# Pooled attention into a feed-forward layer: attention values with tokens in rows and a DMA transpose of x, instead of features in rows

## The chip, the core and the metric

The kernel runs on one core of one Trainium2 chip. The metric is the device time of one execution in microseconds. A core has TensorE (PE, matmul; its weight loads are listed apart as PEld), VectorE (DVE), ScalarE (ACT), GpSimd (POOL), and SyncE (SP), which here only issues DMAs. Matmul results land in PSUM; everything else that the engines read and write lies in SBUF. Sixteen DMA engines move data between the main memory and SBUF, and within SBUF.

## The reference

`q`, `k`, `v` are float32 of shape (8 batches, 8 heads, 576 tokens, 64). Keys and values are averaged over groups of 8 tokens, so each query attends to 72 pooled positions. The attended heads are laid side by side as `x` (4608 tokens x 512) and go through a feed-forward layer with an unusual gate.

```python
k_p = k.reshape(B, H, Sp, pool, D).mean(axis=3)      # pool = 8, Sp = 72
v_p = v.reshape(B, H, Sp, pool, D).mean(axis=3)
scores = scale * np.matmul(q, k_p.transpose(0, 1, 3, 2))
scores = scores - np.max(scores, axis=-1, keepdims=True)
attn = np.exp(scores)
attn = attn / (np.sum(attn, axis=-1, keepdims=True) + 1e-09)
x = np.matmul(attn, v_p)            # then heads side by side: (4608, 512)
h = x @ w_in                        # (4608, 2048)
out = (h * np.cos(h)) @ w_out       # (4608, 512)
```

## The kernel before

**Stages.** The feed-forward layer works on tiles of 512 tokens, the attention on batches of 576. A loop over t = 0..8 (L524) does for tile t the *up* part (x times `w_in`, L317), the gate h cos h (cosine on ACT at L327, product on DVE at L331) and the *down* part (times `w_out`, L395), and between the pieces of the down part the attention of batch b = t + 1. Since a tile is shorter than a batch, the attention runs ahead of the tiles by an amount that shrinks by 64 tokens a stage. The last 64 tokens of a batch (`REST`) are done one stage later than the others. In stage t = 0 down and attention are interleaved by an older list; from t = 1 on the down part is seven products (`down_products`, L367) of 16 matmuls with 256 columns each, held in the two PSUM tiles `obanks`. Batches from the third on (b = 2 to 7, stages t = 1 to 6) are what `steady` marks, and only they are touched by the change.

**Order.** The whole order is written by hand (`manual_schedule`): each engine runs its instructions in the order of the program text, and waits for what it needs. PE, ACT, DVE, POOL and SP each have one such queue. SP issues, in this order in a stage: the output rows of the tile before (8 DMAs), the transposes of q and of the pooled keys, `q_transpose` (L195) and `k_transpose` (L182). POOL issues the loads of the next batch (L95, L114), held back by a one-element copy (`gate`, L662) until the transpose of the keys has landed, and then sums groups of 8 tokens (`pool_add`, L145).

**Attention in a stage, before.** Four groups u0 to u3, each 256 tokens x 4 heads (`BY_TOKENS`), and the REST group of batch t, 64 tokens x 8 heads.

- `scores_mm` (L215): for each head a matmul with the pooled keys (64 x 72) as the stationary operand and q^T (64 x tokens) as the moving one. Heads are ordered so that two neighbours use the two halves of the array's rows. `scores_exp` (L226) takes the exponential on ACT into `ex`, 72 pooled positions x 1024 columns, in bf16. The largest score isn't subtracted.
- `values` (L245): for each head the stationary operand is `vz`, 72 x 128: 64 columns of pooled values and 64 columns that all hold the constant 8, in the order (v, 8) for even heads and (8, v) for odd ones. The moving operand is `ex`. So 64 rows of the result hold the features of the head and 64 rows hold 64 copies of the sum of the exponentials (L251, bank `pair`). ACT takes Ln of the sums (L257, twice) and Exp of minus that (L258), which is the reciprocal; DVE multiplies the two halves (L262, twice) straight into `xT`, which is x with features in rows (128 rows x 4 x 4608 tokens), as the up part needs it.

The constant is 8 since the pooled values are sums, not means, and the factor cancels.

**When xT is read.** The up part of a stage begins with the first two of the four blocks of features for its first two banks (L528, L529: `k0 = 0, k1 = 2`, 8 matmuls) and takes the other two blocks afterwards. The PSUM tiles `banks[0..2]` serve scores, values and the up part in turn.

**Shared buffers.** The reciprocals lie in the tile of `inverse_tile` (L241), 128 x 512 float32, with three buffers in turn.

Of the kernel before, what the change touches and what calls it, by code (L numbers as in the profile page):

```python
# [9 lines left out]
FP32 = mybir.dt.float32  # L10
BF16 = mybir.dt.bfloat16
# [9 lines left out]
def kernel(  # L21
# [9 lines left out]
    nc = tc.nc  # L31
    B, H, S, D = q.shape
    Sp = S // POOL
    d_model = H * D
# [3 lines left out]
    KCH = d_model // 128  # L38
# [8 lines left out]

    SEG = ((0, 256), (256, 256), (512, 64))
    REST = (SEG[2], (0, H))
    BY_TOKENS = [(SEG[s], (4 * j, 4)) for s in range(2) for j in range(2)]  # L50
    BY_HEADS = [(SEG[s], (4 * j, 4)) for j in range(2) for s in range(2)]

    ctx.enter_context(tc.manual_schedule())

# [4 lines left out]
    asb = ctx.enter_context(tc.tile_pool(name="asb", bufs=2))  # L59
# [5 lines left out]
    xT = wpool.tile([128, KCH, n_tokens], BF16, name="xT")  # L65
# [13 lines left out]
    vz = [wpool.tile([Sp, KCH, 4, D], BF16, name=f"vz{i}") for i in range(2)]  # L79
# [3 lines left out]
    banks = [psum.tile([128, 2, 512], FP32, name=f"bank{i}") for i in range(3)]  # L83
# [49 lines left out]
    att = {}  # L133
# [72 lines left out]
    def ex_col(u, i):  # L206

        (c0, n), (h0, nh) = u
        return (i // 2 % 2 * (nh // 2) + i // 4 * 2 + i % 2) * n
# [31 lines left out]
    def inverse_tile(w):  # L241
        inv = asb.tile([128, 512], FP32, name="inv", tag="inv", bufs=3)
        return inv[:, 0:w]

    def values(b, u, pair, later=None):  # L245

        (c0, n), (h0, nh) = u
        ex = att.pop(("ex", b, u))
        for i in range(nh):
            pj, hp = divmod(h0 + i, 2)  # L250
            nc.tensor.matmul(pair[:, hp, (i // 2) * n:(i // 2 + 1) * n],  # L251
                             lhsT=vz[b % 2][:, pj, 2 * hp:2 * hp + 2, :].rearrange("p a d -> p (a d)"),
                             rhs=ex[:, ex_col(u, i):ex_col(u, i) + n])
        w = nh * n // 2
        inv = inverse_tile(w)
        for hp in range(2):
            nc.scalar.activation(out=inv[half[1 - hp]], in_=pair[half[1 - hp], hp, 0:w], func=ACTF.Ln)  # L257
        nc.scalar.activation(out=inv, in_=inv, func=ACTF.Exp, scale=-1.0)  # L258

        def mul():  # L260
            for hp in range(2):
                nc.vector.tensor_mul(out=x_out(b, u, half[hp]), in0=cols(pair[half[hp], hp, :], u),  # L262
                                     in1=cols(inv[half[1 - hp]], u))

        if later is None:
            mul()
        else:
            later.append(mul)

    def sums_first(b, u, cs):  # L270

# [173 lines left out]
    for rows in half:  # L445
# [12 lines left out]
                  for x in (g1, g2)]  # L458
    groups = g3.rearrange("p f n -> p (f n)")[:, 0:ROW * Sp].rearrange("p (t n) -> p t n", t=ROW)
    nc.vector.tensor_tensor(out=dist, in0=row_of.unsqueeze(2).to_broadcast([128, ROW, Sp]),  # L460
                            in1=first_of.unsqueeze(1).to_broadcast([128, ROW, Sp]), op=mybir.AluOpType.subtract)
# [32 lines left out]
    us = BY_HEADS  # L494
# [29 lines left out]
    for t in range(NT):  # L524
        b = t + 1
        if t > 0:

            for fp in up_order(t)[0:2]:  # L528
                up_mm(t, fp, 0, 2)  # L529
        for n, fp in enumerate(up_order(t)):  # L530
            up_mm(t, fp, 2 if n < 2 else 0)
            between = ()
            if t == 0:
                if fp == 4:
                    puts = pool_k_mm(1, obanks[0], 0, 2), pool_k_mm(1, obanks[1], 2, 4)
                elif fp in (5, 6):
                    g0 = 9 * (fp - 5)
                    puts = q_transpose_mm(1, obanks[0], g0, g0 + 5), q_transpose_mm(1, obanks[1], g0 + 5, g0 + 9)
                if fp in (4, 5, 6):
                    puts[0](vec)  # L540
                    between = ((puts[1], act),)
            up_g(t, fp, between)
            if 0 < t and 3 <= n < 6:
                put_gs(*[(k, 0) for k in (((3,), (1,), ()) if t == 1 else ((1, 2), (3,), (4,)))[n - 3]])
            if 0 < t and b < B:
                if n == 0:
                    q_transpose(b)
                elif n == 2:
                    k_transpose(b)
        mms = [(ms, fc) for ms in range(4) for fc in range(FFCH)]  # L550
        if t == 0:
            mms = [(ms, fc) for hm in range(2) for cg in (0, 2, 1, 3) for ms in range(2 * hm, 2 * hm + 2)
                   for fc in range(4 * cg, 4 * cg + 4)]


        def S_(n, bank):
            return lambda: scores(b, us[n], banks[bank])

        later = []

        def V_(n, bank, wait=None):
            return lambda: values(b, us[n], banks[bank], wait)

        fill = []
        if t < B:
            exp_tables()
            fill = [(1, lambda: scores(t, REST, banks[2])), (16, lambda: values(t, REST, banks[1]))]
        if t == 0:
            fill = [(2, fill[0][1]), (2, S_(0, 0)), (8, lambda: pool_v_mm(1, banks[1])),
                    (8, lambda: values(t, REST, banks[2])), (8, S_(1, 0)), (8, V_(0, 1)),  # L570
                    (18, S_(2, 2)), (21, V_(1, 0, later)), (26, S_(3, 1)), (32, lambda: later.pop()()),
                    (32, V_(2, 2)), (40, V_(3, 0))]
        if t < FIRST:
            fi = 0
            for n, (ms, fc) in enumerate(mms):
                while fi < len(fill) and fill[fi][0] <= n:
                    fill[fi][1]()
                    fi += 1
                down_mm(obanks[ms % 2], ms, fc)
                if fc == FFCH - 1:  # L580
                    down_out(t, ms, obanks[ms % 2])
                if n == 4:
                    put_weights(0, nc.vector, (1,))
                elif n == 36:
                    put_weights(1, nc.vector, (3,))
            put_weights(1, nc.vector, (2, 4))
        else:
            products, reads = down_products(t)

            def product(i, j=0, k=2 * HF):  # L590
                for mm in products[i][j:k]:
                    mm()

            us = BY_TOKENS
            later = []

            u0, u1, u2, u3 = [(b, us[i], banks[j]) for i, j in enumerate((2, 1, 0, 1))]
            ur = (t, REST, banks[2])

            def scores_of(*parts):  # L600
                for part in parts:
                    scores_mm(*part)
                for part in parts:
                    scores_exp(*part)

            def muls():
                while later:
                    later.pop(0)()

            steady, rest = b < B, t < B  # L610
            if rest:
                exp_tables()
            product(0)
            product(1, 0, 2)
            if steady:
                scores_of(u0, u1, u2)
            elif rest:
                scores_of(ur)
            product(1, 2)
            if t == 1:  # L620
                put_g(2, 0)
            put_gs((1, 1), (2, 1))
            reads[0]()
            put_g(3, 1)
            reads[1]()
            if t == 1:
                put_g(4, 0)
            if steady:
                values(*u0, later)
            product(2)  # L630
            reads[2]()
            muls()
            if steady:
                values(*u1, later)
            product(3)
            reads[3]()
            muls()
            put_g(4, 1)
            if steady:
                values(*u2, later)  # L640
            product(4)
            reads[4]()
            muls()
            if steady:
                scores_of(ur, u3)
            product(5, 0, 4)
            if rest:
                values(*ur, later)
            product(5, 4, 12)
            muls()  # L650
            if steady:
                values(*u3, later)
            product(5, 12)
            reads[5]()
            muls()
            product(6)
            reads[6]()
        if t < B:
            sin_tables()
        if 0 < t and b + 1 < B:  # L660

            nc.gpsimd.tensor_copy(out=gate, in_=kk[b % 2][0:1, 0, 0:1])  # L662
        if b + 1 < B:
            load_kv(b + 1, "k", k)
            load_q(b + 1)
            load_kv(b + 1, "v", v)
            if t == 0:
                put_weights(0, nc.gpsimd, (3, 2, 4))
                put_weights(1, nc.gpsimd, (1,))
            pool_add(b + 1, "k")  # L670
            pool_add(b + 1, "v")
# [28 lines left out]
```

The softmax here doesn't subtract the row's maximum and nothing guards it: scores larger than these inputs give would overflow.

## Time and profile before

The time is 290.83 us, the median of 3 runs (290.38 to 291.13). The profiled execution has a span of 289.3 us at the full TensorE clock.

| Group | Engine | Count | Busy us | Mean of one, ns |
|---|---|---|---|---|
| up, 128x512 (L317, `bank`) | PE | 512 | 113.9 | 379 |
| cosine (L327, `bank`) | ACT | 64 | 70.3 | 1114 |
| gate product (L331, `bank`) | DVE | 64 | 77.2 | 1220 |
| product into xT, 64x512 (L262) | DVE | 56 | 38.6 | 689 |
| Ln of the sums, 64x512 (L257) | ACT | 56 | 33.1 | 592 |
| Exp of minus Ln, 128x512 (L258) | ACT | 28 | 17.7 | 630 |
| values, 256 columns (L251) | PE | 112 | 16.9 | 272 |
| exp of scores, 72x1024 (L229) | ACT | 32 | 31.0 | 1013 |
| scores, 256 columns (L222) | PE | 128 | 10.9 | 275 |

How to read it: the mean time of a matmul is its whole passage through the array, and the next one starts long before it ends, so the means of PE rows add up to more than the time that passes. What a matmul costs is the distance from its start to the start of the next. ACT and DVE do one instruction after the other, so their rows add up. The stages t = 2 to 6 start their up parts at 83.6, 113.8, 143.5, 173.2 and 202.9 us. In the stage from 143.47 to 173.18 us DVE is busy for 26.34 us, ACT for 24.30, POOL for 20.56.

The DMAs of SP in a stage (times are the length of the issue): output rows 8 x some 0.6 us, q transpose 2.8 us, key transpose 1.2 us; median times from issue to landing are 2.4, 4.9 and 2.8 us.

### The profile page before, as it was taken

Reading aid. Unit: us, or ns where it says so; the run is one execution under the profiler, and the core shown is the slowest. Engines: PE = TensorE matmul, PEld = TensorE weight load, DVE = VectorE, ACT = ScalarE, POOL = GpSimd, SP = SyncE. Lnnn points to the kernel's source line nnn. Section 1 sums busy time; section 2 is a strip of 40 time slices with the busy share of each in tenths; the row PEclk is TensorE's granted clock in tenths of the full one; section 3 lists DMA queues with packets and bytes.
Section 4 is the critical chain, followed back from the end, with each engine's and each line's share of the span. In section 5 each row is a group of like instructions: output and inputs, shape, how many; then the busy total and the mean of one; then the engine's idle time right before and its main releaser. Section 6 shows DMA issues by size and latency. Waiting matters only on the chain.

```text
span 289.3 us, 5446 instructions
## 1 busy us (share of the span) xinstructions
PE 281.1 (97%) x2168; PEld 178.5 (62%) x2168; DVE 233.1 (81%) x314; ACT 208.0 (72%) x265; POOL 149.9 (52%) x145
## 2 busy tenths in 40 slices
PE   7889999999999999999999999999999999999994
PEld 3545554446864587458745884588448854884583
DVE  5558747899988988798979897989798979855972
ACT  3786798378887798679967997699759976436600
POOL 8563079996698379836983599339920000000000
PEclk9999999999999999999999999999999999999999
DMA  7999999554939692969196916694670060006014
GB/s 161 194 206 207 206 205 213 116 107 58 174 72 168 99 162 42 199 92 162 19 196 95 174 31 150 109 169 71 147 106 0 5 144 1 2 5 143 0 39 109
DMA packets 44489, 32.97 MB, mean 114 GB/s; under 512 B 22192, under 2 KB 40112, under 8 KB 44464
## 3 DMA queue, kind: packets, MB, share of 16 engines
q0 software_dynamic: 19744, 18.07, 39.8%
q1 hardware_dynamic: 24080, 14.03, 23.7%
q10 hardware_dynamic: 640, 0.52, 0.7%
q8 instruction: 17, 0.28, 0.4%
q14 instruction: 8, 0.07, 0.1%
HBM read 36.70 MB, written 9.44 MB: 159 GB/s over the span
## 4 chain that ended last, share of the span: by engine, by line
PE 70%; DVE 3%; ACT 0%; issue 0%
PE obank L395 31%; PE bank L317 27%; PE bank L251 4%; PE obank L317 4%; PE bank L222 3%; DVE g_sb L331 2%; PE bank L395 2%; DVE g L361 1%; ACT cos L327 0%; DVE o_two L411 0%
## 5 line engine op out<-in xcount | busy, mean ns | idle before, releaser
L317 PE MATMUL bank<-xT,w_in_sb 128*128 128x512 bf16 x512 | 113.9, 379 | 0.0
L327 ACT ACTIVATE cos<-bank,half_pi 128x1024 f32<-128x1024 f32 x64 | 70.3, 1114 | 46.5 <-PE bank L317 46.5
L317 PEld LDWEIGHTS <-w_in_sb 128*128 128x128 bf16 x576 | 56.1, 98 | 66.0 <-issue 0.6
L331 DVE TENSOR_TENSOR g_sb<-bank,cos 128x1024 bf16<-128x1024 f32 x64 | 77.2, 1220 | 21.0 <-ACT cos L327 20.9
L151 POOL TENSOR_TENSOR half_sums<-kv_st 72x512 f32<-72x512 bf16 x48 | 54.5, 1162 | 26.2 <-DMA kv_st<-in_k_dram 25.8
L395 PEld LDWEIGHTS <-g 128*128 128x128 bf16 x512 | 49.0, 98 | 7.1 <-issue 1.4
L262 DVE TENSOR_TENSOR xT<-bank,inv 64x512 bf16<-64x512 f32 (+1 forms) x72 | 45.3, 629 | 6.8 <-ACT inv L258 5.3
L257 ACT ACTIVATE inv<-bank 64x512 f32<-64x512 f32 (+1 forms) x72 | 39.2, 544 | 10.4 <-PE bank L251 9.4
L395 PE MATMUL obank<-w,g 128*128 128x256 bf16 x368 | 43.6, 272 | 0.0
L395 PEld LDWEIGHTS <-g_sb 128*128 128x128 bf16 x384 | 36.8, 98 | 7.8 <-issue 1.2
L229 ACT ACTIVATE ex<-bank 72x1024 bf16<-72x1024 f32 (+1 forms) x40 | 35.0, 929 | 1.9 <-PE bank L222 1.7
L153 POOL TENSOR_TENSOR half_sums<-half_sums 72x512 f32<-72x512 f32 x24 | 31.8, 1345 | 0.0
L395 PE MATMUL obank<-w_out_sb,g_sb 128*128 128x256 bf16 x240 | 28.9, 273 | 0.3 <-DVE g_sb L331 0.3
L361 DVE TENSOR_TENSOR g<-g_sb 128x1024 bf16<-128x1024 bf16 x32 | 23.7, 740 | 0.5
L258 ACT ACTIVATE inv<-inv 128x512 f32<-128x512 f32 (+1 forms) x36 | 21.0, 583 | 1.1
L251 PE MATMUL bank<-ex,vz 72*128 72x256 bf16 (+1 forms) x176 | 20.0, 243 | 0.1
L156 POOL TENSOR_TENSOR kp<-half_sums 72x512 bf16<-72x512 f32 x12 | 16.4, 1389 | 0.5
L251 PEld LDWEIGHTS <-vz 72*128 72x128 bf16 x176 | 13.6, 97 | 3.5 <-DVE xT L262 0.5
L395 PE MATMUL obank<-w_out_sb,g 128*128 128x256 bf16 x112 | 15.6, 273 | 0.0
L334 PE MATMUL obank<-w_out_sb,g_sb 128*128 128x512 bf16 x64 | 15.3, 379 | 0.2 <-DMA w_out_sb<-in_moe_w_out_dram 0.2
L395 PE MATMUL obank<-w,g_sb 128*128 128x256 bf16 x128 | 15.3, 273 | 0.0
L317 PE MATMUL obank<-xT,w_in_sb 128*128 128x512 bf16 x64 | 15.1, 379 | 0.0
(85 smaller groups left out, 246.2 us busy)
## 6 DMA issues: line engine op xcount, KB each, us to landing
out_dram<-o_two SPq DMA_DIRECT2D x64, 128.0 KB, 2.4
kv_st<-in_v_dram POOLq DMA_DIRECT2D x8, 576.0 KB, 12.9
kv_st<-in_k_dram POOLq DMA_DIRECT2D x7, 576.0 KB, 7.6
q_b<-in_q_dram POOLq DMA_DIRECT2D x6, 576.0 KB, 9.9
w_in_sb<-in_moe_w_in_dram POOLq DMA_DIRECT2D x4, 512.0 KB, 13.6
w_out_sb<-in_moe_w_out_dram POOLq DMA_DIRECT2D x4, 512.0 KB, 19.0
q_b<-in_q_dram POOLq DMA_DIRECT2D x4, 288.0 KB, 12.3
g_sb<-in_k_dram SPq DMA_DIRECT2D x1, 576.0 KB, 3.6
```

Of the source, the lines that this page charges most:

```text
L151: add(out=s[:, h:h + 2], in0=x[:, h:h + 2, 0:4, :], in1=x[:, h:h + 2, 4:8, :], op=ADD)
L153: add(out=s[:, h:h + 4, 0:2, :], in0=s[:, h:h + 4, 0:2, :], in1=s[:, h:h + 4, 2:4, :], op=ADD)
L229: nc.scalar.activation(out=ex[:, 0:nh * n].rearrange("p (a n) -> p a n", a=2), in_=pair[:Sp, :, 0:nh * n // 2], func=ACTF.Exp, scale=scale ...
L251: nc.tensor.matmul(pair[:, hp, (i // 2) * n:(i // 2 + 1) * n], lhsT=vz[b % 2][:, pj, 2 * hp:2 * hp + 2, :].rearrange("p a d -> p (a d)"), ...
L257: nc.scalar.activation(out=inv[half[1 - hp]], in_=pair[half[1 - hp], hp, 0:w], func=ACTF.Ln)
L258: nc.scalar.activation(out=inv, in_=inv, func=ACTF.Exp, scale=-1.0)
L262: nc.vector.tensor_mul(out=x_out(b, u, half[hp]), in0=cols(pair[half[hp], hp, :], u), in1=cols(inv[half[1 - hp]], u))
L317: nc.tensor.matmul(h[j] if h is obanks else h[:, j, :], lhsT=w_in_sb[fc // 4][:, ki, (fc % 4) * 128:(fc % 4 + 1) * 128], rhs=xT[:, ki, t * ...
L327: nc.scalar.activation(out=c, in_=ps, func=ACTF.Sin, bias=half_pi[:, :1])
L331: nc.vector.tensor_mul(out=o, in0=ps, in1=c)
L361: nc.vector.tensor_tensor(out=out[:, f0:f1], in0=x, in1=y, op=op)
L395: mms.append(lambda bank=bank, first=first, g=g, w=w, fc=fc, p=p: nc.tensor.matmul(bank[p], lhsT=g(fc, p), rhs=w(fc), start=(first and fc ...
```

## The change

From the third batch on, the four groups are chunks of 128 tokens with all 8 heads (`CHUNKS`), and the values product is turned around: the exponentials (72 x 128 tokens) become the stationary operand, and the values of the head with *one* column of the constant (72 x 65) the moving one. The result has tokens in rows: per head 64 features and one sum. The reciprocal of the sums is then a DVE instruction over 8 columns, the division is one DVE product of 128 x 512 with the reciprocal broadcast along the features, and neither needs ACT. The price of the layout is that x comes out as 128 tokens x 512 features in bf16, while the up part wants features in rows, so each chunk is transposed by a DMA on SP into `xT`. It is for less work on PE (the 64 copies of each sum are no longer streamed), on ACT and on DVE.

Slices: for an odd head the columns of `vz` are (8, v), so the slice begins at the last constant column (`hp * (3 * D - 1)`), and the sums of a pair of heads come to lie side by side in columns 64 and 65. The 8 heads fill four places of 256 columns in the two PSUM banks. The bf16 chunk takes a buffer of `inverse_tile`. REST keeps the old way (`values`), as do the first two batches.

```diff
-    BY_TOKENS = [(SEG[s], (4 * j, 4)) for s in range(2) for j in range(2)]
     BY_HEADS = [(SEG[s], (4 * j, 4)) for j in range(2) for s in range(2)]
+    CHUNKS = [((128 * i, 128), (0, H)) for i in range(4)]
...
+    def values_rows(b, u, pair):
+
+        (c0, n), (h0, nh) = u
+        ex = att.pop(("ex", b, u))
+        ps = pair.rearrange("p b n -> p (b n)").rearrange("p (j w) -> p j w", w=2 * 128)
+        for i in range(nh):
+            pj, hp = divmod(i, 2)
+            v_and_sum = vz[b % 2].rearrange("p j a d -> p j (a d)")[:, pj, hp * (3 * D - 1):hp * (3 * D - 1) + D + 1]
+            nc.tensor.matmul(ps[0:n, pj, hp * (D + 1):(hp + 1) * (D + 1)], lhsT=ex[:, ex_col(u, i):ex_col(u, i) + n],
+                             rhs=v_and_sum)
+        inv = asb.tile([128, KCH, 2], FP32, name="inv_rows", tag="inv_rows", bufs=2)
+        nc.vector.reciprocal(out=inv[0:n], in_=ps[0:n, :, D:D + 2])
+        x = inverse_tile(512).bitcast(BF16)[:, 0:d_model]
+        nc.vector.tensor_tensor(
+            out=x[0:n].rearrange("p (j a d) -> p j a d", j=KCH, a=2),
+            in0=ps[0:n, :, 0:2 * (D + 2)].rearrange("p j (a w) -> p j a w", a=2)[:, :, :, 0:D],
+            in1=inv[0:n].unsqueeze(3).to_broadcast([n, KCH, 2, D]), op=mybir.AluOpType.mult)
+        nc.sync.dma_start_transpose(out=xT[:, :, b * S + c0:b * S + c0 + n], in_=x[0:n])
...
-            us = BY_TOKENS
...
-            u0, u1, u2, u3 = [(b, us[i], banks[j]) for i, j in enumerate((2, 1, 0, 1))]
+            u0, u1, u2, u3 = [(b, CHUNKS[i], banks[j]) for i, j in enumerate((2, 1, 0, 1))]
...
             if steady:
-                values(*u0, later)
+                values_rows(*u0)
             product(2)
             reads[2]()
             muls()
...
```

The other three groups change from `values` to `values_rows` in the same way, u1 ahead of product 3, u2 ahead of product 4, u3 ahead of the last four matmuls of product 5. The old form put its products on DVE behind the next read (`later`, `muls`); the new form puts its two DVE instructions right behind its matmuls in the program, ahead of that read.

More of the change, by code (lines that the diff above doesn't have):

```diff
@@ L633 @@
             if steady:
-                values(*u1, later)
+                values_rows(*u1)
             product(3)
@@ L639 @@
             if steady:
-                values(*u2, later)
+                values_rows(*u2)
             product(4)
@@ L651 @@
             if steady:
-                values(*u3, later)
+                values_rows(*u3)
             product(5, 12)
```

## The prediction

> **What bounds the kernel now.** I read the page's table of engines first, then the chain of work that ended last for one steady stage, then the TensorE timeline around the values. The first gives the suspect:
>
> ```profile
> PE 281.1 (97%) x2168; PEld 178.5 (62%) x2168; DVE 233.1 (81%) x314; ACT 208.0 (72%) x265; POOL 149.9 (52%) x145
> ```
>
> PE is busy 97% of the span, but busy is no proof, since matmuls overlap. The chain, cut to stage t=4 (143.47 to 173.18 us), is the proof:
>
> ```profile
> 143.47 5.18 PE bank L317 x24
> 148.65 1.73 PE obank L317 x8
> 150.38 6.91 PE bank L317 x32
> 157.28 1.97 PE obank L395 x18
> 159.25 0.91 PE bank L222 x12
> 160.16 1.63 PE obank L395 x14
> 161.79 0.44 PE bank L251 x4
> 162.23 1.75 PE obank L395 x16
> ...
> 168.35 0.48 PE bank L222 x12
> 168.83 0.54 PE obank L395 x4
> 169.37 0.31 PE bank L251 x8
> ```
>
> Each piece begins where the last one ended, all on PE: no wait on this chain, and the stage lasts what its matmuls take, 29.71 us. L317 is up, L395 down, L222 scores, L251 values. So a saving on PE counts in full, one on ACT or DVE counts nothing, and the only way to lose is a new wait in front of a matmul. The timeline gives the start times that I price with:
>
> ```profile
> 169.29 0.39 PE L251 MATMUL bank<-ex,vz 72*128 72x64 bf16 x8
> 169.52 1.04 PE L395 MATMUL obank<-w_out_sb,g 128*128 128x256 bf16 x8
> 170.40 0.60 PE L251 MATMUL bank<-ex,vz 72*128 72x256 bf16 x4
> 170.84 0.60 PE L395 MATMUL obank<-w_out_sb,g 128*128 128x256 bf16 x4
> ```
>
> The second column overlaps with the next row; the difference of starts is the cost. Eight values matmuls with 64 columns and a 72x128 stationary load each take 169.52 - 169.29 = 0.23 us, 29 ns apiece; four with 256 columns take 170.84 - 170.40 = 0.44 us, 109 ns apiece.
>
> **What the skill says.** (1) "TensorE: Matmul & The Clock Gate", section Back-to-back issue gap: a warm matmul costs N/2.4 + 2.5 ns (109 for 256 columns), with about 60 cycles, 25 ns, up to 64 columns. The trace agrees (109 and 29). The same section says streams with a weight load per matmul at N=128 hold about 81 ns; the eight at 29 ns with a 128-column load each contradict that as a floor here. (2) "VectorE: DVE Perf Modes", section The TRN2 errata: an fp32 tensor_tensor takes (N+151)/0.96 ns, 691 at 512; the trace has 692. (3) "DMA: Bandwidth & Descriptors", section Queues, rings and completion order: an engine takes turns between queues, packet by packet. Trace, 49 to 51 us: q0 moved 140 packets and q1 158, while outputs issued beside loads landed after 5.2 us (45 to 54 us), against 2.4 us alone. (4) Same page, section Rules for kernel authors: a transpose next to ordinary DMAs needs no serialization, so I expect no extra wait for that; the trace of before keeps its transposes apart from loads and can't say.
>
> **The change, part by part**, for each of the six stages t=1..6.
>
> *Values on PE.* Out: 16 matmuls of 256 columns, 16 x 109 = 1.74 us. In: 4 chunks x 8 heads of 65 columns with 128-column stationary loads, at the 29 ns of the near-identical row, 32 x 29 = 0.93 us. Saved: 0.81. Bounds on the pitch: 29 from below; from above 54 ns (109/2), were the load of ex to bind, which would save nothing.
>
> *Scores on PE.* 16 matmuls of 256 columns become 32 of 128, running in pairs on two row halves: the same 4096 columns. Pairs of 256 start 109 ns apart in steady flow; twice the pairs cost 8 more fixed parts of 2.5 ns, +0.02 us. Upper bound +0.1.
>
> *ACT.* Out: per group two Ln (592 ns) and one Exp (630 ns), 4 x 1.81 = 7.3 us a stage. ACT is not on the chain: worth 0. exp(scores) keeps its 72x1024 form.
>
> *DVE.* Out: 8 products of 64x512 at 689 ns, 5.51 us. In: 4 products of 128x512 at 692 plus 4 reciprocals of 8 elements, priced between (8+151)/0.96 = 166 ns and 0.25 us: 3.4 to 3.8 us. About 2 us less, hidden behind PE. The new ops don't wait for ACT, so they finish earlier. Queued behind the reciprocal are the reads of obanks; in t=4 the first read after it idled 1.07 us for its product before, so they have room.
>
> *SP and DMA.* In: 4 transposes of 128x512. The q transpose (18 blocks) issues in 2.84 us and lands after 4.9, kk (8 blocks) in 1.24 and 2.8. By line: 0.155 us issue per block, landing 1.1 + 0.21 per block. A chunk of 4: 0.62 us issue, 2.0 us to landing in quiet. Behind the last chunk on SP stand the outputs and the next q and kk transposes; they come about 1.3 us later relative to the stage. kk landed at S+10.7 (S = start of up; in t=3 the copy that waits for kk runs at 124.51, up starts at 113.76), so now S+12, and scores need it at S+15.5: hidden. The next loads also start 1.3 us later; POOL idled 3.9 us for kk and 4.9 us for k in t=4, so its sums still come in time.
>
> *The new wait.* The next up reads xT of all features at its start; the old one needed only the first four heads for the first 1.7 us. Which chunks it needs follows from 512-token tiles against 576-token batches: 0 to 2 for t=1 and 2; 0 and 1 for t=3 and 4; 0 for t=5 and 6; never chunk 3. In t=2: values of chunk 2 leave PE at about 106.4, DVE does read, put_g and then the new pair by about 108.7, quiet landing 110.7 to 111.3; up starts at 113.76 - 0.75 = 113.0. Slack about 2 us. Chunk 1 has 2.2 us more.
>
> *REST* still goes through ACT. Its product ended at 112.86 before, for an up at 113.76; PE gains only 0.21 us between its values and up, so 0.7 us remain.
>
> **Sum.** 6 x (0.81 - 0.02) = 4.7. In t=1 the product behind the first values starts at 72.52, just after a DVE read of 71.78 + 0.68 = 72.46 frees its bank; there 0.2 is lost. 290.8 - 4.5 = **286.3 us**.
>
> **The rivals.**
> (a) *Contended transposes*, 288.3. Loads run from 95.6 to about 110 in t=2 (the last is issued at 97.17 and takes some 12.5), right where the chunks move. The queue view gives 22 ns per 256-byte transpose packet (151 to 154 us: 107.1% of 16 engines over 3 us, 2293 packets) and 110 ns per load packet (158 to 164 us: 113.5%, 992). A chunk is 512 packets, 32 per engine; one for one with loads it takes 32 x 132 = 4.2 us instead of 0.7. They queue behind each other, and chunk 2 would land about 1 us late in t=1 and 0.8 late in t=2, chunk 1 of t=3 and 4 just in time: +2 us. For: the one-for-one count above. Against: several transpose rows may go per turn.
> (b) *Up waits for the last chunk too*, 301. Chunk 3's product ends near S+0.4 and lands near S+2.5. If the wait of up on xT doesn't tell tokens apart, each stage loses 2.5: 286.3 + 15. Against: nothing on the chain of before shows such a wait, but there the last write also came early enough for the second half of features to hide one.
> (c) *The short matmuls don't get short*, 290.9: at 54 ns because ex as stationary or a 65-column operand that starts at an odd element costs more than the row with vz. Against: same rows, columns and type.
>
> **How the numbers follow.** Forecast 0.61, (a) 0.20, (b) 0.10, (c) 0.09. The forecast with its unknowns (scores +0.1, pitch 29 to 33) spans 285.5 to 287.7; (a) reaches 289.6 if chunk 1 is late as well. 285.5 to 289.6 leaves out (b) and (c), 0.19. Faster by over 0.3% (under 289.96): 0.61 + 0.19 + 0.01 = 0.81; slower: (b) and a fifth of (c), 0.12; the rest 0.07.
>
> **What would show it.** Right: values matmuls 29 ns apart, stages of about 28.9 us, a chain still on PE without waits, ACT busy down by some 43 us, and transposes landing before up. PE idle before L317 with the DMA as releaser is (a) in stages 1 to 4 alone, (b) in all six. A pitch near 54 ns is (c). I am wrong above all if the first up matmul of a stage waits.

## The result and the profile after

The changed kernel takes 302.74 us (median of 4 runs, 300.30 to 303.59) against 290.87 before; the ratio is 1.0396, with a 95% interval of 1.0330 to 1.0463. All ratios are against the kernel before, run beside each version. It is slower by about 12 us; 286.3 was forecast, with 285.5 to 289.6 as the range. Line numbers in the profile after: up is L336 (was L317), down L414 (L395), values in the new form L278, the reciprocal L281, the product L283, the transpose of x L287. REST's Ln, Exp and product keep L257, L258, L262.

The page's first row and the shares of its chain:

```profile
PE 280.5 (93%) x2360; PEld 177.5 (59%) x2360; DVE 219.2 (73%) x314; ACT 164.4 (55%) x193; POOL 150.2 (50%) x145
...
PE 61%; DMA 9%; ACT 2%; issue 1%; DVE 1%; ACTq 0%
```

ACT is down by 43.6 us, as priced (6 x 7.3), and DVE by 13.9, a little more than priced (6 x 1.7 to 2.1); none of it helps. The new entry is DMA in the chain, 9%, which before held PE and little else. Where it stands is seen in the chain of stage t=3 (start, length, what):

```profile
135.06 0.25 PE bank L278 x8
135.31 1.76 PE obank L414 x16
137.07 0.01 issue
137.08 9.77 DMA xT<-inv
146.84 0.02 issue
146.86 0.04 ACTq L257
146.90 0.04 issue
146.95 0.38 ACT inv L257
147.32 0.01 issue
147.34 0.39 ACT inv L257
147.72 0.02 issue
147.75 0.43 ACT inv L258
148.17 0.02 issue
148.20 0.04 DVE xT L262
148.24 0.39 issue
148.62 0.44 DVE xT L262
149.06 0.04 issue
149.11 7.02 PE bank L336 x24
```

The transpose of chunk 0 is issued at 137.08 and lands 9.77 us later. What then starts is not up, but the Ln of REST on ACT (L257). It writes a reciprocal into a tile of `inverse_tile`, which has three buffers in turn; chunks 0, 1 and 2 took all three, and REST's turn falls on the one from which the transpose of chunk 0 is still reading. Ln, Exp and REST's product follow in a row, and up, which reads REST's tokens, comes last. Before, the groups u0, u1 and u2 took the same three buffers; REST's turn then fell on one whose last reader was a DVE product, done some 4 us earlier. ACT's timelines of that stage, before and after, show it (a bracket is idle time before, and what ended it):

```profile
140.46 0.77 ACT L257 ACTIVATE inv<-bank 64x256 f32<-64x256 f32 x2
```

```profile
146.95 0.77 ACT L257 ACTIVATE inv<-bank 64x256 f32<-64x256 f32 x2 [4.10 <-DMA xT<-inv]
```

PE's timeline after shows the other end:

```profile
143.09 0.41 PE L278 MATMUL bank<-vz,ex 72*128 72x65 bf16 x8
143.34 0.60 PE L414 MATMUL obank<-w_out_sb,g 128*128 128x256 bf16 x4
143.78 1.91 PE L414 MATMUL obank<-w,g_sb 128*128 128x256 bf16 x16
149.11 1.44 PE L336 MATMUL bank<-xT,w_in_sb 128*128 128x512 bf16 x3 [3.42 <-DVE xT L262]
```

REST's values had been ready since 142.4 or so, and PE idles 3.42 us for them. In t=4 and 5 the trace names the same releaser of the Ln. In t=1 and 2 it names another, but the Ln starts at 83.23 and 114.41 us, 0.08 and 0.07 us after chunk 0's landing at 83.15 and 114.34, so it is the same wait. The first two rows also give the price of the new matmuls: 143.34 - 143.09 = 0.25 us for eight, 31 ns each.

Stage by stage, from start of up to start of up in the trace:

| Stage | Before, us | After, us | Difference | After: last down matmul to next up, start to start, us |
|---|---|---|---|---|
| t=1 | 29.92 | 31.69 | +1.77 | 2.46 |
| t=2 | 30.13 | 31.19 | +1.06 | 2.34 |
| t=3 | 29.71 | 32.53 | +2.82 | 3.69 |
| t=4 | 29.71 | 33.37 | +3.66 | 2.85 |
| t=5 | 29.71 | 31.97 | +2.26 | 1.44 |
| t=6 | 29.71 | 28.95 | -0.76 | 0.1 |

In t=6 there is no next batch to load; its four transposes land after 2.4 to 2.8 us, and the stage lasts what was forecast. Stages 4 and 5 lose more than the idle time. The table of windows (length; busy PE, PEld, DVE, ACT, POOL with counts; granted TensorE clock, where 1.00 is full speed; DMA share, GB/s) shows why, for t=3 to t=6 and for the first 3.41 us of t=4:

```profile
116.57:149.11 32.54, 29.12 (x257) 19.42 (x257) 24.19 (x35) 17.06 (x20) 21.82 (x21) 1.00 0.87 127
149.11:182.47 33.36, 30.79 (x256) 19.79 (x256) 23.78 (x35) 17.04 (x20) 21.25 (x20) 0.95 0.85 124
182.47:214.44 31.97, 30.80 (x256) 19.80 (x256) 24.05 (x35) 17.05 (x20) 20.28 (x20) 0.95 0.84 129
214.44:243.56 29.12, 29.12 (x257) 19.48 (x257) 23.74 (x36) 17.41 (x20) 7.67 (x7) 1.00 0.41 81
149.12:152.53 3.41, 3.41 (x9) 1.18 (x9) 2.06 (x4) 0.34 (x1) 3.41 (x4) 0.50 0.23 43
```

The same matmuls are busy 30.8 us instead of 29.1, at a mean granted clock of 0.95. It stood at 0.50 for 3.4 us, from 149.12 in t=4 and from 183.25 in t=5, and the first 24 matmuls of up took 7.02 us, where 5.34 is usual after a wait. Both followed the two longest waits (PE idle for 3.42 and 2.58 us); after 2.19 and 2.07 us the clock stayed at 1.00. That the waits are the cause fits, but with two cases of each it isn't shown whether their length decides or their place in time. These two stages give 2 x 1.7 = 3.4 of the 10.9 us by which the span grew; the rest is waiting, less the saving.

### The profile page after: what moved, and what is told of

Its sections match the earlier page's. It is cut to its first block, busy times and chain, and to the rows that moved or that the text cites. A ratio compares the mean times of both kernels' runs of the same rounds, so it can differ in the third digit from the quotient of the medians.

```text
span 300.2 us, 5861 instructions
## 1 busy us (share of the span) xinstructions
PE 280.5 (93%) x2360; PEld 177.5 (59%) x2360; DVE 219.2 (73%) x314; ACT 164.4 (55%) x193; POOL 150.2 (50%) x145
## 4 chain that ended last, share of the span: by engine, by line
PE 61%; DMA 9%; ACT 2%; issue 1%; DVE 1%; ACTq 0%
PE bank L336 30%; PE obank L414 23%; DMA xT<-inv 9%; PE obank L336 4%; PE bank L222 2%; PE bank L414 2%; ACT inv L257 1%; PE bank L278 1%; DVE xT L262 1%; ACT inv L258 1%; PE bank L251 0%; DVE o_two L430 0%; ACTq L257 0%
## 5 line engine op out<-in xcount | busy, mean ns | idle before, releaser
L336 PE MATMUL bank<-xT,w_in_sb 128*128 128x512 bf16 x512 | 117.2, 387 | 11.4 <-DVE xT L262 11.4
L336 PEld LDWEIGHTS <-w_in_sb 128*128 128x128 bf16 x576 | 56.9, 99 | 80.6 <-issue 14.9
L350 DVE TENSOR_TENSOR g_sb<-bank,cos 128x1024 bf16<-128x1024 f32 x64 | 77.3, 1221 | 27.1 <-ACT cos L346 27.1
L151 POOL TENSOR_TENSOR half_sums<-kv_st 72x512 f32<-72x512 bf16 x48 | 56.1, 1194 | 26.6 <-DMA kv_st<-in_k_dram 26.1
L414 PEld LDWEIGHTS <-g 128*128 128x128 bf16 x512 | 47.5, 98 | 5.9 <-issue 0.3
L414 PE MATMUL obank<-w,g 128*128 128x256 bf16 x368 | 43.6, 272 | 0.2 <-DVE p_sb L428 0.2
L414 PEld LDWEIGHTS <-g_sb 128*128 128x128 bf16 x384 | 36.8, 98 | 6.7
L262 DVE TENSOR_TENSOR xT<-bank,inv 64x256 bf16<-64x256 f32 (+1 forms) x24 | 12.3, 511 | 28.7 <-ACT inv L258 28.4
L153 POOL TENSOR_TENSOR half_sums<-half_sums 72x512 f32<-72x512 f32 x24 | 30.8, 1301 | 0.0
L414 PE MATMUL obank<-w_out_sb,g_sb 128*128 128x256 bf16 x240 | 28.7, 273 | 0.0
L257 ACT ACTIVATE inv<-bank 64x256 f32<-64x256 f32 (+1 forms) x24 | 10.8, 450 | 22.5 <-DMA xT<-inv 9.2
L283 DVE TENSOR_TENSOR inv<-bank,inv_rows 128x512 bf16<-128x512 f32 x24 | 16.6, 692 | 0.8
L414 PE MATMUL obank<-w_out_sb,g 128*128 128x256 bf16 x112 | 15.6, 273 | 0.0
L414 PE MATMUL obank<-w,g_sb 128*128 128x256 bf16 x128 | 15.3, 273 | 0.0
L380 DVE TENSOR_TENSOR g<-g_sb,g 128x1024 bf16<-128x1024 bf16 x16 | 15.2, 951 | 0.0
L336 PE MATMUL obank<-xT,w_in_sb 128*128 128x512 bf16 x64 | 15.1, 379 | 0.0
L680 POOL COPY gate<-kk 1x1 bf16<-1x1 bf16 x5 | 1.4, 280 | 23.8 <-DMA kk<-kp 23.8
```

What stands on the lines that cost most here:

```text
L151: add(out=s[:, h:h + 2], in0=x[:, h:h + 2, 0:4, :], in1=x[:, h:h + 2, 4:8, :], op=ADD)
L153: add(out=s[:, h:h + 4, 0:2, :], in0=s[:, h:h + 4, 0:2, :], in1=s[:, h:h + 4, 2:4, :], op=ADD)
L283: nc.vector.tensor_tensor(out=x[0:n].rearrange("p (j a d) -> p j a d", j=KCH, a=2), in0=ps[0:n, :, 0:2 * (D + 2)].rearrange("p j (a w) -> ...
L336: nc.tensor.matmul(h[j] if h is obanks else h[:, j, :], lhsT=w_in_sb[fc // 4][:, ki, (fc % 4) * 128:(fc % 4 + 1) * 128], rhs=xT[:, ki, t * ...
L350: nc.vector.tensor_mul(out=o, in0=ps, in1=c)
L380: nc.vector.tensor_tensor(out=out[:, f0:f1], in0=x, in1=y, op=op)
```

## The experiments

The theory that this profile suggests, **W**: loads make the transposes late, and the late transpose of chunk 0 stops the stage *through the buffer* that REST's Ln needs. Its rivals: **L**, the buffer is a bystander and up waits for its chunks of xT themselves; and **T**, transposes of x are slow in any case.

### e1: own buffers

```diff
-        x = inverse_tile(512).bitcast(BF16)[:, 0:d_model]
+        odd = c0 // n % 2
+        if not odd:
+            att["x", b] = inverse_tile(512).bitcast(BF16)
+        x = att["x", b][:, odd * d_model:(odd + 1) * d_model]
```

> The changed kernel, but the chunks of x no longer share a buffer with the reciprocals of REST: two chunks lie in one tile, so that REST's Ln gets a buffer whose last reader is a stage old. Theory W (late transposes stop the stage through the buffer: REST's Ln waits until the transpose of chunk 0 has read it) expects the Ln never to wait for a DMA and up to start when the chunks it needs have landed; from the landings in the changed kernel that is 1.3, 0.7, 1.3, 1.8 and 2.3 us earlier in t=1 to 5, and with shorter idle of PE the clock stays full in t=4 and 5 (another 3.4): 292 to 296 us. Rival L (up waits for its chunks of xT themselves, the buffer is a bystander) expects 301 to 304, no change.

Measured: 291.56 us, ratio 1.0017 (1.0004 to 1.0030), a little below the 292 to 296 expected. Eleven of the twelve microseconds are gone with the buffers apart, with the transposes as slow as before (median landing 5.0 us, against 4.9; 7.5 to 9.1 for chunk 0 in t=1 to 5). ACT's Ln waits for no DMA any more, and the clock is 1.00 in all six stages. L is out as the main cause. What L says is true only of the rest, as the chain of t=4 shows:

```profile
164.52 1.35 PE obank L417 x13
165.87 8.77 DMA xT<-inv
174.64 0.14 issue
174.77 1.24 PE bank L339 x5
```

The transpose of chunk 1, issued at 165.87, lands at 174.64, and up (L339 here) starts right behind it. In t=1 and 2 up follows chunk 2 (84.28 and 84.42; 113.88 and 114.12), in t=3 chunk 1 (143.45 and 143.49; DVE's product of chunk 3 ends at the same moment, so the two can't be told apart there), in t=5 nothing. Those are the chunks that the tiles of 512 need; chunk 3 landed 1.4 to 4 us after up had begun in t=1 to 3, so no wait on it exists.

### e2: loads left out, after and before

```diff
             load_kv(b + 1, "k", k)
-            load_q(b + 1)
-            load_kv(b + 1, "v", v)
+            staged["q", b + 1] = staged["q", 1]
+            staged["v", b + 1] = staged["k", b + 1]
```

> The changed kernel with two of three loads left out from batch 2 on: only k is loaded, the values are pooled from the k tile and q of batch 1 is used for every later batch. The transposes of x then meet no load. If loads are what makes the transposes late (theories W and L alike), each lands in about 2.4 us as in stage t=6 of the changed kernel, nothing waits, and the time is that of the forecast, 286 to 287 us, even with the shared buffer. If transposes of x are slow or late by themselves, it stays above 296.

> Control: the kernel before with the same two loads left out in the same way. PE bounds it without waits, so every theory expects 290.5 to 291.2 us; a smaller time would mean that loads cost the kernel before something, and would have to be taken off the run with the changed kernel.

Both kernels leave out two loads, so their output is not that of the reference. Measured: 287.70 us with the change (ratio 0.9887, 0.9868 to 0.9907), 0.7 above the 286 to 287 expected, and 291.24 without it (0.9998, 0.9989 to 1.0008). With the shared buffer untouched, the transposes land on time (count and median landing in us, in the changed kernel and here):

```profile
xT<-inv SPq DMA_TRANSPOSE x24, 4.9
```

```profile
xT<-inv SPq DMA_TRANSPOSE x24, 2.4
```

and the chain of t=4 is matmuls again, with nothing between them:

```profile
159.56 0.25 PE bank L278 x8
159.81 1.75 PE obank L414 x16
161.56 0.25 PE bank L278 x8
161.81 1.75 PE obank L414 x16
163.56 0.25 PE bank L278 x8
163.80 1.75 PE obank L414 x16
165.55 0.48 PE bank L222 x16
```

T is out: loads are the root. Stages 2, 4 and 6 last 28.95 us here. Stages 3 and 5 last 29.52 and 29.94, since in each PE waits twice for a gate product of DVE (L350), late in the up part and right behind it. POOL's sums come at another time in this kernel and meet DVE there, as its timeline and POOL's show for t=3:

```profile
120.54 1.43 DVE L380 TENSOR_TENSOR g<-g_sb 128x1024 bf16<-128x1024 bf16 x1
```

```profile
120.15 1.26 POOL L159 TENSOR_TENSOR vz<-half_sums 72x512 bf16<-72x512 f32 x1
```

The DVE sum, 0.69 us where it is alone, ends 0.56 us after POOL's (121.97 and 121.41), as if it had run only then. The gate products behind it are pushed back, and these two stages lose 1.6 us against 28.95. Stage 1 lasts 29.58, with two short waits for reads of DVE.

How the loads delay a transpose is seen in the queues of the changed kernel (kind: packets, MB, share of 16 engines). First 137 to 140 us, just after chunk 0 was issued at 137.08:

```profile
q0 software_dynamic: 456, 0.50, 110.9%
```

No packet of the transposes' queue q1 runs in these three microseconds. Then 142 to 146 us:

```profile
q1 hardware_dynamic: 740, 0.18, 78.8%
q0 software_dynamic: 325, 0.33, 53.0%
```

Now the two queues share the engines; a chunk has 544 packets, nearly all of 256 bytes, so 740 in 4 us are a chunk and a third. A chunk pays for a late first packet and for shared engines, and the second is the larger part. In t=1 to 5 the first packet of chunk 0 came 1.8, 3.5, 3.4, 2.3 and 1.2 us after the issue, against 1.2 in t=6 without loads; from there to the landing it took 6.0, 4.9, 6.3, 6.7 and 6.2 us, against 1.3. In these stretches 1077 to 1457 packets of q1 ran, so later chunks moved before the first had landed. Why the first packet takes up to 3.5 us beside loads, and whether chunk 0 waits for the packets of later chunks too, was not tested.

### e3 and e5: new form only where it may be late

```diff
+            us = CHUNKS if t >= 6 else BY_TOKENS[0:2] + CHUNKS[2:4] if t >= 3 else BY_TOKENS
...
-                values_rows(*u0)
+                values_of(u0)
```

Here `values_of` takes `values_rows` for a chunk and `values` for a group of the old form; the buffers are apart as in e1.

> Own buffers as above, and the new form of values only for chunks that the next up doesn't read while loads are running: none in t=1 and 2, chunks 2 and 3 in t=3, 4 and 5 (groups 0 and 1 stay in the old form), all four in t=6. Late landings are then harmless. Theory W with contention as its root expects the saving on PE to show, 10 chunks x 0.19 us = 1.9: 288.7 to 289.4 us. If late transposes cost by another way too (what stands behind them on SP: outputs, next q and k transposes), it is 291 or more.

Measured: 290.48 us, 0.9970 (0.9958 to 0.9983): faster than before, but a third of what was expected. Stages 3 to 5 saved nothing. Their chain turns from PE to DVE ahead of product 6 (L418):

```profile
139.61 0.22 DVE inv_rows L282
139.83 0.02 issue
139.85 0.06 DVE inv L287
139.92 0.05 issue
...
140.46 0.69 DVE o_two L434
141.15 0.04 issue
141.19 1.91 PE obank L418 x16
```

Product 6 adds into a bank that DVE must read first (L434), and ahead of that read DVE now does chunk 2's reciprocal and product, on top of the old products of groups 0 and 1, which still come later in these mixed stages. e5 moves the pair and the transpose behind the read:

```diff
+        def mul():
             inv = asb.tile([128, KCH, 2], FP32, name="inv_rows", tag="inv_rows", bufs=2)
             nc.vector.reciprocal(out=inv[0:n], in_=ps[0:n, :, D:D + 2])
...
+        later.append(mul)
```

> As e3 (own buffers, new form for late chunks only), but the two DVE instructions of a chunk and its transpose come behind the next read of a product's bank, as the old products did. In e3 the product that follows waited 0.3 to 0.4 us for a read of DVE in each of t=3, 4 and 5 (twice in 5), since the new pair stood ahead of it. If that order is why e3 saved only 0.6 us where 1.9 were expected, the waits go and the time is 288.9 to 289.5 us. If the matmuls of mixed stages save less by themselves, it stays at 290.3 or more.

Measured: 289.52 us, 0.9930 (0.9903 to 0.9957), at the upper end of what was expected. The waits ahead of product 6 are gone, and stages 4 and 5 last 29.40 and 29.41 us, 0.3 less than before; t=3, with 29.74, lost 0.3 us to a product into xT on DVE early in its up part. So the order on DVE was the cause in t=3 and 4. In t=5 some of the gain has another reason: a bf16 sum on DVE that took 1.71 us beside POOL in e3 took 0.75 here. The same meeting cost this version something in t=6, which lasts 29.34 us against 28.96 in e3: a sum in the up part took 1.25 us beside POOL, and PE waited for the gate product behind it. The version is faster than the kernel before and than the changed one.

### e4, e6 and e7: the load of v moved

```diff
             load_kv(b + 1, "k", k)
             load_q(b + 1)
-            load_kv(b + 1, "v", v)
-            pool_add(b + 1, "k")
+            pool_add(b + 1, "k", None if t == 0 else lambda: load_kv(b + 1, "v", v))
```

The load is then issued in the middle of POOL's sums of k.

> Own buffers for the chunks as in e1, and the load of v moved: POOL issues it in the middle of its sums of k, some 12 us later, so that the chunks' transposes fall into a gap between loads (stage t=0 stays). If what is left of the loss in e1 (PE idle ahead of up by 1.6, 0.9, 0.4 and 2.0 us in t=1 to 4) is the landing of chunks under the loads, those gaps go except for some 1 us in t=1 and perhaps t=2, where chunk 2 is needed and still meets v: 286.5 to 288 us. If it isn't the loads but the queue of transposes behind each other on SP, it stays at 291 to 292.

> The changed kernel with its shared buffer, and only the load of v moved as in e4. If the shared buffer costs only because the transpose of chunk 0 is late, an early landing frees it in time and nearly all of the 12 us goes: 287 to 290 us. If the shared buffer stops the stage even with transposes on time, it stays above 296.

> Control: the kernel before with the load of v moved in the same way. No transpose of x, no wait on PE's chain: 290.5 to 291.3 us by every theory. Over 291.5 would mean that the late load costs by itself (POOL or v not in time).

Measured: 294.97 with own buffers (1.0131, 1.0084 to 1.0179), 294.95 with the shared one (1.0125, 1.0062 to 1.0187), 297.37 for the control (1.0205, 1.0152 to 1.0259). All three times lie outside what was forecast, for the reason that the expectation of the control names: the move costs some 6 us by itself. Without the control, e4 would have read as evidence against loads. Most of it is seen on DVE in the control (t=3 and t=4):

```profile
140.17 2.66 DVE L363 TENSOR_TENSOR g<-g_sb,g 128x1024 bf16<-128x1024 bf16 x1
...
170.99 3.23 DVE L363 TENSOR_TENSOR g<-g_sb,g 128x1024 bf16<-128x1024 bf16 x1
```

This sum of bf16 tiles takes 0.68 us mostly, and a matmul of product 5 waits for it. It grew to 2.7 and 3.2 us where POOL issues the load of v (138.88 and 170.28) and then sums; in t=4 POOL's two sums behind the load run from 171.16 to 173.66 and the DVE sum ends 0.56 us later. In e4 and e6 other sums of DVE, in the up parts, meet POOL in the same way.

Against the control, the change gains 2.4 us in both buffer arrangements by the medians, but the runs of one version spread by 2.6 to 4.1 us and the intervals overlap, so this is not clear of noise. What the traces show stage by stage is of more use. In e4 no up waits for a chunk. In e6 chunk 0 landed after 5.5, 7.0, 7.3, 6.2 and 7.0 us in t=1 to 5, against 7.4 to 9.8 in the changed kernel. In the three stages with 7.0 and more the shared buffer still stopped up, by 0.56, 0.92 and 0.69 us; in t=1 and 4 it did not. In t=3:

```profile
144.14 1.02 PE L338 MATMUL bank<-xT,w_in_sb 128*128 128x512 bf16 x4 [0.92 <-DVE xT L264]
```

That fits W: the buffer costs what the landing is late. The equal medians of e4 and e6 don't show that it is free, as e4 lost more in its up parts.

### e8: a mixed version

```diff
-            us = CHUNKS if t >= 6 else BY_TOKENS[0:2] + CHUNKS[2:4] if t >= 3 else BY_TOKENS
+            us = CHUNKS if t >= 5 else BY_TOKENS[0:2] + CHUNKS[2:4] if t >= 3 else BY_TOKENS
```

From t=5 on the DVE pair stands right behind the matmuls as in the changed kernel.

> As e5 in t=1 to 4 (old form in t=1 and 2, new form for chunks 2 and 3 in t=3 and 4, DVE pair behind the read), and all four chunks in the new form from t=5 on with the pair right behind the matmuls, as in e1, where t=5 lost nothing and lasted 28.95 us. If the stages are independent of each other, 0.4 us is won over e5 in each of t=5 and 6: 288.5 to 289.1 us. If the transposes of t=5 are late here, it is 289.5 or more.

Measured: 289.39 us, 0.9933 (0.9908 to 0.9957), between the two ranges expected and the same as e5 within the intervals. The transposes of t=5 were in time (chunk 0 landed at 200.90, up at 201.84), but t=5 lasted 29.37 us and t=6 29.56, with PE waits of 0.3 to 0.4 us for gate products of DVE in the up part and at its end. Ahead of them a bf16 sum of DVE took 1.28 us in t=5 and 1.48 in t=6 beside a sum of POOL; in t=5 of e5 the same sum took 0.69. So the stages are not independent, and the second half of the expectation named the wrong reason.

## Why the prediction was wrong

- **What bounds the kernel** held: the chain was PE without waits (but in t=2, whose chain runs through cosines and gate products from 88.85 to 99.08 us; it lasted 30.13), less work on ACT and DVE was worth nothing, and the only way to lose was a new wait ahead of a matmul. That way was taken.
- **Values and scores on PE** held: 31 ns instead of 29 for a matmul of 65 columns, scores unchanged (0.91 and 0.48 us for the two groups in both chains), and 0.76 us saved where nothing waits (t=6), against 0.79. Rival (c) is out.
- **DVE and ACT** held: 692 ns and some 0.2 us for the pair. What was left out is what a DVE sum takes beside POOL; it did not decide this result, but it limited e2, e5 and e8.
- **The step that failed is "REST still goes through ACT ... so 0.7 us remain".** It followed REST's chain through engines and never asked what REST's Ln *writes into*. REST comes fourth in a rotation of three buffers, so its Ln waits for the last reader of chunk 0's buffer, and that reader had become a DMA. That the x chunk takes `inverse_tile` was in the diff, and the buffers were not counted. In place of 0.7 us to spare, PE idled 1.2 to 3.4 us ahead of up in t=1 to 5. Own buffers (e1) gave back 11 of the 12 us.
- **The term that was mis-sized** is the landing of a transpose. In quiet 2.4 us came, where 2.0 was worked out, and the issue took 1.2 us instead of 0.62: the line through the q and key transposes doesn't hold for four blocks. Beside loads rival (a) had 4.2 us of moving and a fixed part of 1.1 for chunk 0; 7.4 to 9.8 came: up to 2.4 us of it because the first packet came late, and 4.9 to 6.7 us for the moving. With buffers in order rival (a) would have been near the truth in kind: e1 lost to chunk 2 in t=1 and 2 and to chunk 1 in t=4 (in t=3 perhaps), stages that it named, but by 1.5, 0.7, 2.0 and 0.4 us, where 1, 0.8 and nothing were worked out. Point (4) of the prediction, no serialization, says what must be ordered and nothing of the time.
- **Rival (b)** came close to the time, 301, by accident: up never waited for chunk 3, which e1 shows to land after up had begun. An all-stages loss was expected of it; t=6 gained.
- A cost that no case held: the lower clock behind the two longest waits, 3.4 us.

## What to carry to other kernels

When a DMA takes the place of an engine as the reader of a tile, its buffer is held until the landing: count the buffers of that rotation against the *latest* landing, and look for who writes into them next. A transfer that was measured in a quiet stretch must be priced for the stretch in which it will run, and a control of the kernel before with the same edit is what keeps such a test honest. Here the DVE work of the new form did best behind the reads that free PE's banks where old and new form were mixed (e5, t=3 and 4). And sums of bf16 tiles on DVE are worth keeping away from sums on POOL.

## What was not expected of the hardware

- A transpose of 128x512 issued beside loads landed after 7.4 to 9.8 us for chunk 0, against 2.4 us in quiet, and its first packet ran up to 3.5 us after the issue. The skill's turns packet by packet ("DMA: Bandwidth & Descriptors", section Queues, rings and completion order) fit the later stretch in so far as both queues moved, though 740 packets to 325 are not one for one; they leave the first stretch open, in which q1 had none.
- A bf16 sum of 128x1024 on DVE, 0.68 us, took up to 3.4 us in the control while POOL summed and issued a load (up to 1.8 us in the kernel before). The prediction took no account of POOL beside DVE. A reason that fits stands in the skill: "SBUF — State Buffer", section SBUF: two separate sides, says that a DVE instruction with two SBUF inputs and a GpSimd instruction that reads SBUF exclude each other for their whole length. The traces agree: in the eleven runs 97 such sums took over 0.85 us, each ended 0.55 to 0.56 us behind the end of a sum of POOL, and none that met no sum of POOL took over 0.70. DVE products with one operand in PSUM kept their 0.69 us beside the same sums.
- PE waits of 3.42 and 2.58 us were followed by 3.4 us at half the clock, 1.7 us more each for the same matmuls; waits of 1.17, 2.07 and 2.19 us were not.
